# Moving tail loads and zT transposes in SyncE's queue of a fused attention and MLP kernel

## The chip, the cores and the metric

The kernel runs on one core of one Trainium2 chip. The metric is the device time of one execution in microseconds, the median of several runs. The profile is one further execution, recorded by the hardware profiler.

Engines as the profile names them: PE is TensorE (matrix products; PEld are its weight loads), DVE is VectorE, ACT is ScalarE, POOL is GpSimd, SP is SyncE. SyncE computes nothing here: its queue (SPq) issues nearly all DMA transfers, in the order in which they are written. DMA data are moved by 16 DMA engines.

## The reference

Inputs q, k, v have shape (8, 8, 576, 64): batch, heads, sequence, head dimension. All is float32. The output is (8, 576, 512).

```python
scores = scale * np.matmul(q, k.transpose(0, 1, 3, 2))      # scale = 1/sqrt(64)
mask = (rel >= 0) & (rel < 64)                              # rel = query position - key position
attn = softmax(where(mask, scores, -1e9))
x = np.matmul(attn, v)            # heads side by side: (8, 576, 512)
xn = (x - mean) / np.sqrt(var + 1e-6) * g_ln                # over the last axis
out = x + np.maximum(xn @ w_ch1, 0.0) @ w_ch2               # 512 -> 2048 -> 512
```

Each query sees only itself and the 63 keys before it.

## The kernel before, in words

**Blocks and tails.** A batch has 576 rows. Its first 512 are one *block*: blocks 0 to 7, of four sub-blocks of 128 rows (kb 0 to 3). The last 64 rows of two neighbouring batches make one *tail* of 128 rows: tails 0 to 3. The four tails together form a ninth group of 512 rows, number 8 (NGRP - 1), which goes through the MLP like a block.

**Periods.** The main loop (line 963) runs a period g for each of the nine groups. In period g TensorE does the MLP of group g, and between the pieces of that MLP the attention of block b = g + 1 is done and the inputs of block g + 2 are prepared. Period g, from 3 to 6, also does the attention of tail g - 3.

**Units and slots.** The MLP of a period is a list of *units* (`mlp_units`, line 488). In periods 3 to 6 there are 30: units 0 to 15 are layer 1 (four matmuls of 128x512 into a PSUM bank `hps`, then ReLU on ScalarE into `hrT`, line 498); units 16 to 29 are layer 2, computed with seven products of half-size blocks (4, 1, 2, 6, 5, 7, 3; two units each; `product`, line 550, banks pA, pB, pC), whose sums and differences VectorE makes (`s_sums`, line 535). `at(i, f, ...)` puts a step behind unit i; a slot beyond the last (40) means the period's end. The order is written out by hand: all engines take their instructions in this order, and each engine waits at the front of its own queue until what it needs is there. Moving a call moves its instructions within each engine's queue.

**Attention steps.** `s_pe` (line 312) makes the scores of 128 rows on TensorE, `s_exp` the exponential on ScalarE, `s_mask` (360) multiplies by the mask on VectorE, `b_pe` (373) makes the product with v (the tile `xps`), `b_rows` (395) divides by the row sum into `x_norm` (tile `xn`) and takes mean and variance on VectorE, `z_step` (429) normalises to `z` in float16 on GpSimd, and `zt_step` (464) transposes z into `zT`, which layer 1 reads; from block 2 on this is nearly always a DMA transpose from SyncE's queue (470). z has three buffers, so a z that is not transposed yet holds up the third z after it.

**Inputs.** `load_qk` (82), `load_v` (177) and `load_tail` (97) issue loads from SyncE. q and k are cast to float16 on GpSimd (`cast_qk`, 155; in part on ScalarE, `cast_act`, 145) and then transposed: k by TensorE, q of blocks 3 and up by a DMA transpose (`t_main`, 271, line 275). For a tail, `cast_tail` (112) casts tq and tk on GpSimd, `t_tail` (298) issues two DMA transposes into tqT and tkT (302, 303), which the tail's scores read, and `cast_tail_v` (120) casts tv into vt for its product. Loads, transposes and stores share SyncE's queue, so their order in the code is the order in which they are issued.

**Stores.** `store` (532) writes finished rows out from the `xn` buffers: kb 2 and 3 after product 7, kb 0 and 1 after product 3, the last of the period (lines 621 to 634). There are two `xn` tiles to a block and four buffers, so the rows of block g + 2 are written over those of group g: they need its stores to be done.

**The order at the end of a period, before.** At the end of period 4, behind the stores: loads of tail 2's q and k, loads of block 7's q and k; then from slot 2 of period 5: zT of tail 1, the two transposes of tail 2, v of block 7 (first half), tail 2's v, zT of block 6's kb 0.

Of the kernel before, what the change touches and what calls it, by code (L numbers as in the profile page):

```python
# [18 lines left out]
def kernel(  # L19
# [15 lines left out]
    NGRP = B + 1  # L35
# [927 lines left out]
    for g in range(NGRP):  # L963
# [7 lines left out]
        def at(i, f, *a):  # L971
            slots[min(i, len(slots) - 1)].append((f, a))

        def first_scores(b, i):
            at(i, s_pe, b, 0)
            at(i, s_pe, b, 1, False, "xps")
            at(i, s_exp, b, 0, 0, 1)
            at(i + 1, s_exp, b, 1, 0, 1)
            at(i + 1, s_mask, b, 0)
            at(i + 2, s_mask, b, 1)  # L980

        b = g + 1
# [48 lines left out]
        if g == 1:  # L1031
# [38 lines left out]
            for j in range(4):  # L1070
                i = (13, 16, 22, 22)[j]
# [5 lines left out]
                i = (13, 17, 25, 27)[j]  # L1077
# [26 lines left out]
        if g == 2:  # L1104
            at(0, load_qk, 4, 1)
            at(0, s_exp, 3, 1, 1)
            at(1, z_act, 2, 3)
            at(1, s_mask, 3, 1)
            at(2, b_pe, 3, 0)
            at(2, s_pe, 3, 2)  # L1110
            at(2, s_pe, 3, 3, False, "t")
            at(5, zt_step, 2, 3, "act")
            for i, x in zip((2, 3, 4, 6), ((3, 0), (3, 1), (2, 0), (2, 1))):
                at(i, s_exp, 3, *x)
            at(3, load_v, 4, 0, 4)
            at(4, s_mask, 3, 3)
            at(4, b_rows, 3, 0)
            at(4, z_step, 3, 0)
            at(7, s_mask, 3, 2)
            at(7, alloc_qkT, 4)  # L1120
            at(7, after_mask, 3, 2)
            at(7, cast_qk, 4, 0)
            at(7, cast_qk, 4, 1)
            for j in range(1, 4):
                at(9, b_pe, 3, j, ("xps", "t", "sc")[j - 1])
                at((9, 10, 11)[j - 1], b_rows, 3, j)
                at((9, 10, 11)[j - 1], z_step, 3, j)
            for j, i in enumerate((8, 14, 24, 25)):
                at(i, zt_step, 3, j)
        elif g > 1 and b < B:  # L1130
            r, i = NGRP - 1, g - 3
            x, y = (b, 3), (r, i)
            if g > 3:
                at(2, zt_step, r, i - 1)
            at(2, b_pe, b, 0)
            at(2, b_rows, b, 0)
            at(2, z_step, b, 0)
            if g > 4:
                at(2, cast_tail, i)
                at(2, t_tail, i)  # L1140
            if g == 5:
                at(2, load_v, 7, 0, 2)
                at(2, load_tail, 2, "v")
            at(2, s_pe, b, 2)
            at(2, s_exp, b, 2, 0, 1)
            at(3, s_mask, b, 2)
            at(2, s_pe, *x, False, "t")
            at(4, s_exp, *x, 0)
            at(5, s_exp, *x, 1)
            at(5, s_mask, *x)  # L1150
            at(7, b_pe, b, 1)
            at(7, b_pe, *x, "t")
            at(7, b_rows, b, 1)
            at(7, z_step, b, 1)
            at(8, b_rows, *x)
            at(9, z_step, *x)
            at(13, b_pe, b, 2)
            i_s = 13 if g == 6 else 17
            at(i_s, s_pe, *y)
            at(i_s + 2 if g == 6 else i_s, s_exp, *y, 0, 1)  # L1160
            if g == 6:
                at(15, s_mask, *y)
                at(18, b_pe, *y, "sc")
            else:
                at(20, s_mask, *y)
            if g + 2 < B:
                at(5, alloc_qkT, g + 2)
                at(5, after_mask, *x)
                at(5, cast_qk, g + 2, 0)
                at(11, cast_qk, g + 2, 1, (0,))  # L1170
                at(15, cast_act, g + 2, 1, 1)
            for j, w in ((13, (b, 2)), (19, y)) if g == 6 else ((17, (b, 2)),):
                at(j, b_rows, *w)
                at(j, z_step, *w)
            at(2, zt_step, b, 0)
            at(14, zt_step, b, 1)
            if g == 6:
                at(25, zt_step, r, i)
            at(16, zt_step, b, 3)
            at(18 if g == 6 else 17, zt_step, b, 2)  # L1180
        n = g + 2
        if g > 1 and n < B:
            if g > 2:
                at(3, load_v, n, 2, 4)
            at(17, alloc_v, n)
            at(17, cast_v, n, 0, 2)
            at(17, cast_v, n, 2, 4)
            if g == 2:
                at(26, part_vB, n, 0, 4)
            else:  # L1190
                at(17, alloc_vB, n)
                for i, f, c in ((18, vB_cur, 0), (18, vB_prev, 0), (19, vB_cur, 1), (19, vB_prev, 1),
                                (24, vB_cur, 2), (24, vB_prev, 2), (24, vB_cur, 3)):
                    at(i, f, n, c, 0)
            for i, (x, half) in zip((13, 18, 13, 22) if g == 2 else (13, 17, 13, 23),
                                    ((0, 0), (1, 0), (0, 1), (1, 1))):
                at(i, t_main, n, x, half, 0)
            if g > 2:
                at(23, b_pe, NGRP - 1, g - 3, "sc")
                at(23, b_rows, NGRP - 1, g - 3)  # L1200
                at(23, z_step, NGRP - 1, g - 3)
            first_scores(n, 27)
            if n + 1 < B:
                if g == 2:
                    at(40, t_tail, 0)
                elif g == 4:
                    at(40, load_tail, 2, "q")
                    at(40, load_tail, 2, "k")
                at(40, load_qk, n + 1, 0)
                at(40, load_qk, n + 1, 1)  # L1210
                if g == 3:
                    at(40, t_tail, 1)
                if g < 4:
                    at(40, load_v, n + 1, 0, 2)
                if g == 3:
                    at(40, load_tail, 1, "v")
            else:
                for part in "qkv":
                    at(40, load_tail, g - 2, part)
# [4 lines left out]
        if 2 < g < NGRP - 2:  # L1224
            for i in range(1, 5):
                at(7 + i, s_sums, 0, 4, i)
                at((13, 13, 19, 19)[i - 1], s_sums, 4, 6, i)
                at((15, 15, 20, 22)[i - 1], s_sums, 6, 8, i)
        if g in (2, 3):
            for part in "qkv"[:5 - g]:  # L1230
                at(15 if g == 2 else 17, load_tail, g - 2, part)
            at(24, cast_tail, g - 2)
        if 3 <= g < 7:
# [8 lines left out]
        if g in (6, 7):  # L1242
            i = 25 if g == 6 else 24
# [40 lines left out]
```

## Time and profile before

| what | value |
|---|---|
| median of 3 runs | 298.48 us (298.47 to 298.74) |
| the profiled execution, its own time | 299.89 us |
| its span in the profile | 298.2 us |
| mean granted TensorE clock | 0.998 |
| busy share of the span: PE, DVE, ACT, POOL | 97%, 76%, 56%, 55% |
| DMA moved | 57.63 MB in 116,519 packets, mean 193 GB/s |
| packets under 512 B | 86,273 |
| period 4 (first layer 1 matmul to that of the next) | 149.96 to 181.02 us |
| period 5 | 181.02 to 214.08 us |

How to read it: a row of the timeline begins with its start and its length in us, then the engine, the line of the kernel, the operation, the tiles (output <- inputs) and the number of instructions that it merges. Brackets at its end give the time that the engine stood idle before, and what it is taken to have waited for. An SPq row's length is the time that SyncE's queue took to issue; landing comes later, and is read from the table of DMA issues (median us from issue to landing). A row of the windows gives the stretch, its length, busy time and instructions of PE, PEld, DVE, ACT and POOL, the granted clock, the mean busy share of the 16 DMA engines, and GB/s. The share can exceed 1 where transfers overlap in an engine.

### The profile page before, as it was taken

The numbers are of one execution on the slowest core, as the hardware profiler recorded it, in microseconds if no ns is written. First come the engines' busy times: TensorE is split into PE (matmuls) and PEld (weight loads), VectorE is DVE, ScalarE is ACT, GpSimd is POOL, SyncE is SP. The second block draws the span as 40 slices with busy tenths as digits, with TensorE's granted clock in tenths as the row PEclk, the third lists the DMA queues.
The fourth block names the chain that finished last, engine by engine and source line by source line (L and its number), as shares of the span: only waits on it lengthen the run. The fifth ranks groups of instructions, "written<-read, shape, count | busy, mean of one in ns | idle before, by whom it ended". The sixth has DMA issues, their size and how long they took to land.

```text
span 298.2 us, 7942 instructions
## 1 busy us (share of the span) xinstructions
PE 290.0 (97%) x3207; PEld 210.4 (71%) x3207; DVE 226.6 (76%) x435; ACT 168.0 (56%) x284; POOL 164.9 (55%) x243
## 2 busy tenths in 40 slices
PE   8989999999999999999999999999999999999994
PEld 3557545898888888447854786458654888888883
DVE  1782378799994894497757786778989898988983
ACT  2667657677449625768576767658575217305500
POOL 4688866753850885268647491693757543104300
PEclk9999999999999999999999999999999999999999
DMA  7999999969989999899699995999887222003013
GB/s 189 259 381 340 385 286 279 264 213 301 159 180 301 249 155 217 222 312 155 136 294 253 172 157 185 263 216 205 168 203 126 55 73 88 4 0 144 0 37 106
DMA packets 116519, 57.63 MB, mean 193 GB/s; under 512 B 86273, under 2 KB 107841, under 8 KB 116482
## 3 DMA queue, kind: packets, MB, share of 16 engines
q1 hardware_dynamic: 116112, 56.79, 79.7%
q8 instruction: 25, 0.41, 0.6%
q10 hardware_dynamic: 370, 0.33, 0.3%
q14 instruction: 12, 0.10, 0.1%
HBM read 38.80 MB, written 9.44 MB: 162 GB/s over the span
## 4 chain that ended last, share of the span: by engine, by line
PE 82%; DMA 7%; DVE 3%; SPq 3%; issue 2%; ACT 1%; POOL 0%; POOLq 0%; DVEq 0%
PE pA L572 14%; PE hps L498 12%; PE hph L641 12%; PE pB L572 9%; PE pC L572 8%; PE lA L697 5%; PE ch L658 4%; PE xps L392 3%; DMA tkT<-tk 3%; PE sc L345 3%; PE tp L286 3%; PE lC L697 2%; PE warm L887 2%; DMA tk<-in_k_dram 2%; DMA qk<-in_k_dram 2%
## 5 line engine op out<-in xcount | busy, mean ns | idle before, releaser
L498 PE MATMUL hps<-zT,w1g 128*128 128x512 f16 x288 | 65.9, 379 | 0.0
L502 ACT ACTIVATE hrT<-hps 128x512 f16<-128x512 f32 x72 | 43.2, 599 | 25.6 <-PE hps L498 20.7
L572 PEld LDWEIGHTS <-sS 128*128 128x128 f16 x512 | 49.1, 98 | 6.0
L355 ACT ACTIVATE pt<-sc 128x512 f16<-128x512 f32 x72 | 39.5, 601 | 17.2 <-PE sc L345 16.7
L498 PEld LDWEIGHTS <-w1g 128*128 128x128 f16 x288 | 27.0, 98 | 31.0 <-issue 1.5
L572 PEld LDWEIGHTS <-hrT 128*128 128x128 f16 x384 | 36.7, 98 | 6.8 <-ACT hrT L502 0.8
L641 PE MATMUL hph<-zT,w1g 128*128 128x256 f16 x320 | 37.9, 273 | 0.0
L365 DVE TENSOR_TENSOR pt<-pt,mask 128x1024 f16<-128x1024 f16 x32 | 24.6, 776 | 14.6 <-ACT pt L355 14.6
L161 POOL CAST qk<-qk 128x1024 f16<-128x1024 f32 x26 | 28.0, 1087 | 11.7 <-PE sc L345 6.0
L444 POOL TENSOR_SCALAR rsz<-mvg 128x1 f32<-128x1 f32 x32 | 11.8, 368 | 40.8 <-DVE mvg L425 38.2
L641 PEld LDWEIGHTS <-w1g 128*128 128x128 f16 x320 | 30.4, 98 | 4.5 <-ACT w1g L238 0.2
L572 PE MATMUL pC<-w2s,sS 128*128 128x256 f16 x256 | 31.5, 273 | 0.0
L572 PE MATMUL pA<-wT,sS 128*128 128x256 f16 x256 | 30.9, 273 | 0.0
L646 ACT ACTIVATE hrT<-hph 128x512 f16<-128x512 f32 x40 | 24.1, 606 | 10.8 <-PE hph L641 10.6
L714 POOL TENSOR_SCALAR hrT<-hrT 128x512 f16<-128x512 f16 x8 | 12.0, 1503 | 28.6 <-DVE hrT L712 28.6
L416 DVE TENSOR_TENSOR xn<-xps,rcp 128x256 f32<-128x256 f32 (+1 forms) x50 | 25.8, 539 | 1.3 <-DMA out_dram<-xn 0.6
L546 DVE TENSOR_TENSOR sS<-hrT 128x1024 f16<-128x1024 f16 (+2 forms) x39 | 23.3, 598 | 3.5 <-ACT hrT L502 3.4
L422 DVE BATCH_NORM_STATS2 stats<-xn 128x6 f32<-128x512 f32 x36 | 25.0, 694 | 1.2
L450 POOL TENSOR_SCALAR z<-xn,rsz 128x512 f16<-128x512 f32 x24 | 21.7, 905 | 6.7 <-DMA zT<-z 4.2
L267 ACT COPY qkT<-tp 128x1024 f16<-128x1024 f16 (+1 forms) x18 | 17.3, 963 | 14.3 <-PE tp L286 12.1
L445 POOL TENSOR_TENSOR rsz<-rsz,mhalf 128x1 f32<-128x1 f32 x32 | 21.5, 671 | 2.7
L189 POOL CAST vA<-v 128x1024 f16<-128x1024 f32 (+1 forms) x18 | 17.4, 981 | 6.0 <-DMA v<-in_v_dram 5.7
(115 smaller groups left out, 484.6 us busy)
## 6 DMA issues: line engine op xcount, KB each, us to landing
qk<-in_q_dram SPq DMA_DIRECT2D x16, 512.0 KB, 6.0
qk<-in_k_dram SPq DMA_DIRECT2D x16, 512.0 KB, 7.6
out_dram<-xn SPq DMA_DIRECT2D x32, 256.0 KB, 2.8
v<-in_v_dram SPq DMA_DIRECT2D x28, 256.0 KB, 5.9
w2s<-in_moe_w_ch_dram SPq DMA_DIRECT2D x9, 512.0 KB, 8.7
w1s<-in_moe_w_ch_dram SPq DMA_DIRECT2D x4, 512.0 KB, 7.3
tk<-in_k_dram SPq DMA_DIRECT2D x8, 256.0 KB, 4.7
tv<-in_v_dram SPq DMA_DIRECT2D x8, 256.0 KB, 5.8
```

Source lines behind the costliest of these rows:

```text
L161: nc.gpsimd.tensor_copy(out=dst[:, :].rearrange("p (a j) e d -> p a e j d", j=j), in_=t[:, :].rearrange("p (a e j d) -> p a e j d", e=2, j ...
L355: nc.scalar.activation(out=o, in_=i, func=AF.Exp, bias=0.0, scale=scale)
L365: nc.vector.tensor_tensor(out=ptv, in0=ptv, in1=mb, op=ALU.mult)
L416: nc.vector.tensor_tensor(out=xn[:, n * i:n * i + n], in0=xps[:, :, 0:D], in1=rcp_b, op=ALU.mult)
L422: nc.vector.bn_stats(out=stats, in_=xv)
L450: nc.gpsimd.tensor_scalar(out=z, in0=xv, scalar1=rs, scalar2=nm, op0=ALU.mult, op1=ALU.add)
L498: nc.tensor.matmul(out=hps, lhsT=w1g[:, kc, 128 * hc:128 * (hc + 1)], rhs=zT[g][:, kc, :], start=(kc == 0), stop=(kc == NKC - 1),)
L502: nc.scalar.activation(out=hrT[:, hc, :], in_=hps, func=AF.Relu, bias=0.0, scale=1.0)
L546: nc.vector.tensor_tensor(out=o, in0=x, in1=y, op=op)
L572: nc.tensor.matmul(out=o, lhsT=a[:, c, 128 * p:128 * p + 128], rhs=wv[:, c, :], start=(first and (p == 0 or split_c) and c == 0), stop=(c ...
L641: nc.tensor.matmul(out=hps[:, e], lhsT=w1g[:, kc, 128 * hc:128 * (hc + 1)], rhs=zT[g][:, kc, 256 * half:256 * half + 256], start=(kc == 0) ...
L646: nc.scalar.activation(out=hrT[:, 2 * i:2 * i + 2, 256 * half:256 * half + 256], in_=hps, func=AF.Relu, bias=0.0, scale=1.0)
```

## The change

Only the order of steps changes; each instruction stays, with the same shapes.

- Loads of tail 2's q and k: from the end of period 4, behind the stores, to slot 17 of period 4, behind the zT of block 5's kb 2 and ahead of the stores. The cast of tail 2's q and k: from slot 2 of period 5 to slot 24 of period 4. Its transposes: from slot 2 of period 5 to the end of period 4, behind block 7's q and k (in the queue this is the same place but for the zT below).
- zT of tail 0, 1 and 2: from slot 2 of the next period to the end of the own one, right behind the stores and ahead of the q and k loads of the next block (of tail 3's loads in period 5).
- In periods 4 and 5, v of the next block (first half) and the tail's v go behind the zT of kb 0, where they stood ahead of it.
- Period 6: product of block 7's kb 2 and scores of tail 3 from unit 13 to unit 15, exponential still at 15, mask from 15 to 17, product of the tail from 18 to 19, its rows from 19 to 20.

```diff
@@ steps of period g (3 to 6)
-            if g > 3:
-                at(2, zt_step, r, i - 1)
...
-            if g > 4:
+            if g == 6:
                 at(2, cast_tail, i)
                 at(2, t_tail, i)
-            if g == 5:
-                at(2, load_v, 7, 0, 2)
-                at(2, load_tail, 2, "v")
...
-            at(13, b_pe, b, 2)
-            i_s = 13 if g == 6 else 17
+            at(15 if g == 6 else 13, b_pe, b, 2)
+            i_s = 15 if g == 6 else 17
             at(i_s, s_pe, *y)
-            at(i_s + 2 if g == 6 else i_s, s_exp, *y, 0, 1)
+            at(i_s, s_exp, *y, 0, 1)
             if g == 6:
-                at(15, s_mask, *y)
-                at(18, b_pe, *y, "sc")
+                at(17, s_mask, *y)
+                at(19, b_pe, *y, "sc")
...
-            for j, w in ((13, (b, 2)), (19, y)) if g == 6 else ((17, (b, 2)),):
+            for j, w in ((15, (b, 2)), (20, y)) if g == 6 else ((17, (b, 2)),):
                 at(j, b_rows, *w)
                 at(j, z_step, *w)
             at(2, zt_step, b, 0)
+            if g in (4, 5):
+                at(2, load_v, g + 2, 0, 2)
+                at(2, load_tail, i, "v")
@@ the end of period g
+            if g > 2:
+                at(40, zt_step, NGRP - 1, g - 3)
             if n + 1 < B:
                 if g == 2:
                     at(40, t_tail, 0)
-                elif g == 4:
-                    at(40, load_tail, 2, "q")
-                    at(40, load_tail, 2, "k")
                 at(40, load_qk, n + 1, 0)
                 at(40, load_qk, n + 1, 1)
-                if g == 3:
-                    at(40, t_tail, 1)
-                if g < 4:
+                if g > 2:
+                    at(40, t_tail, g - 2)
+                else:
                     at(40, load_v, n + 1, 0, 2)
-                if g == 3:
-                    at(40, load_tail, 1, "v")
...
-        if g in (2, 3):
-            for part in "qkv"[:5 - g]:
+        if g in (2, 3, 4):
+            for part in "qkv"[:3 if g == 2 else 2]:
                 at(15 if g == 2 else 17, load_tail, g - 2, part)
             at(24, cast_tail, g - 2)
```

## The prediction

> **What bounds the kernel now.** I read the page first, then TensorE's timeline for periods 4 and 5, then SyncE's and GpSimd's rows in the same stretch, then the windows.
>
> ```profile
> span 298.2 us, 7942 instructions
> PE 290.0 (97%) x3207; PEld 210.4 (71%) x3207; DVE 226.6 (76%) x435; ACT 168.0 (56%) x284; POOL 164.9 (55%) x243
> ```
>
> TensorE is busy for 97%, so only its idle time can be won without taking work away. The timeline shows where that is:
>
> ```profile
> 149.96 2.78 PE L498 MATMUL hps<-zT,w1g 128*128 128x512 f16 x12
> 168.13 0.41 PE L345 MATMUL sc<-tqT,tkT 64*128 64x64 f16 x16
> 174.71 0.45 PE L392 MATMUL xps<-vt,pt 128*64 128x65 f16 x16
> 181.02 2.78 PE L498 MATMUL hps<-zT,w1g 128*128 128x512 f16 x12
> 200.12 0.41 PE L345 MATMUL sc<-tqT,tkT 64*128 64x64 f16 x16 [0.58 <-DMA tkT<-tk]
> 207.04 0.45 PE L392 MATMUL xps<-vt,pt 128*64 128x65 f16 x16 [0.28 <-DVE xn L585]
> 211.70 0.53 PE L345 MATMUL sc<-qkT,qkT 64*128 64x64 f16 x24 [0.38 <-DMA qkT<-qk]
> 214.08 2.79 PE L498 MATMUL hps<-zT,w1g 128*128 128x512 f16 x12
> 229.09 0.41 PE L345 MATMUL sc<-tqT,tkT 64*128 64x64 f16 x16 [0.43 <-DMA tkT<-tk]
> ```
>
> The hps rows open periods 4, 5 and 6. Period 4 takes 181.02-149.96 = 31.06 us, period 5 takes 33.06 us for the same matmuls: 2.00 us to win. Laying one on the other: 0.27 up to unit 13 (VectorE's mask took 0.97 us at 188.72, 0.69 at 157.66), 0.65 at tail 2's scores, 0.34 at its vt product, 0.57 at block 7's scores, 0.16 at the end (period 6's first matmul waits for zT). Period 6 waits 0.51 more for tail 3's keys. The vt wait is charged to VectorE, but GpSimd's cast of vt ended at 206.98, after 4.12 us of waiting for tv.
>
> ```profile
> 173.41 4.32 SPq L470 DMA_TRANSPOSE zT<-z  x3
> 180.05 2.70 SPq L533 DMA_DIRECT2D out_dram<-xn  x4
> 182.80 1.32 SPq L107 DMA_DIRECT2D tq<-in_q_dram  x2
> 184.17 2.38 SPq L110 DMA_DIRECT2D tk<-in_k_dram  x2
> 186.59 1.18 SPq L92 DMA_DIRECT2D qk<-in_q_dram  x1
> ```
> ```profile
> 193.74 2.60 SPq L303 DMA_TRANSPOSE tkT<-tk  x1
> 197.79 3.64 SPq L110 DMA_DIRECT2D tv<-in_v_dram  x2
> 204.90 3.46 SPq L275 DMA_TRANSPOSE qkT<-qk  x2
> ```
> ```profile
> 175.00:180.00 5.00, 5.00 (x81) 4.29 (x76) 4.08 (x9) 3.56 (x6) 4.32 (x7) 1.00 0.47 105
> 200.00:205.00 5.00, 4.88 (x62) 4.42 (x63) 4.16 (x10) 4.78 (x8) 1.52 (x3) 1.00 1.44 203
> ```
>
> SyncE's one queue serves all this. It stands idle from 177.73 to 180.05, held at the stores, while the DMA share (next to last column) is 0.47; from 182.80 it works without a pause, and at 200 to 205 the share is 1.44. Everything late in period 5 is late in this one line.
>
> **The change, part by part.**
>
> *Tail 2's q and k before the stores of period 4.* Four issues (1.32 + 1.25 to 2.38 us) move from behind the stores to behind zT of block 5's block 2. I put that zT's end at 178.1 (next paragraph), so they take the idle SyncE time to 180.7 or 181.8. The first two stores go from 180.05 to about 180.8, the second two still wait for VectorE until 181.94. What followed, block 7's q and k, started at 186.59; now it starts at 182.8 plus one moved zT (1.3 to 1.9 us), 184.1 to 185.2. If DMA throughput, not issue, is the limit, the same backlog of stores and tail starts at 178.1 instead of 180.05: 1.95 us. I take this smaller shift for all that comes later. GpSimd's casts of tail 2 (0.61 and 1.04 us) now stand ahead of block 6's z_0; keys issued at 180.1 land 5.2 us later (the tk row) and are cast by 186.4, about when z_0's statistics are there (186.10): z_0 is late by 0.3 at most, and SyncE asks for it only at 192.
>
> *zT of the tail's rows behind the stores.* In period 4 its z was ready at 148.06, in period 5 about 180.1: no wait. It delays q and k of the next block by its issue, counted above. *zT of the first block ahead of v.* Period 4: two transposes of 1.5 us each now go ahead of v6 and tv1, which start 3 us later; tv1 lands at 172.0 instead of 169.1 (issued at 164.30, 4.8 to land), its cast ends at 173.3, and the vt product starts at 174.71: hidden, with 1.4 us left, else its lateness is paid. In return GpSimd's wait of 4.24 us at 169.79 (z for a buffer that this zT holds) goes; tv1 becomes the next late thing, so z of block 2 ends about 0.4 us later, 176.0, which is where 178.1 comes from. Period 5: it adds 0.6 us of transfer ahead of tv2 and nothing ahead of the transposes of block 7, which it already preceded.
>
> *What period 5 wins*, with the shift of 1.95: tail 2's keys land at 200.07-1.95 = 198.1, wanted at 168.13+31.06 = 199.2 (199.5 if the slow mask stays): 0.65 won. tv2 (second issue at 199.66 at the latest, 5.8 to land) arrives about 205.4-1.95+0.6 = 204.1, is cast in 1.3 by 205.4, and is wanted at 174.71+31.06 = 205.8: 0.34 won. qkT of block 7 lands at 211.6-1.95 = 209.65, wanted at 178.69+31.06 = 209.8: as close as the estimate can tell, 0.50 of 0.57. zT at the end: 0.12 of 0.16. The slow mask had tail 2's q cast beside it on GpSimd (188.54); the cast moves to about 183, z_0 takes its place: 0.14 of 0.27. Sum 1.75; ends 0.65 and 2.00.
>
> One page speaks on that last term. The Trainium skill (SBUF — State Buffer, Who interferes with whom) says that a VectorE instruction with two SBUF inputs contends with a GpSimd one that reads SBUF. The two overlapping rows agree; by it 0.27 would be won if z_0 is over by 188.72, and nothing if not.
>
> *Period 6's tail at unit 15.* Two units are eight matmuls, 1.74 us of cover. But TensorE comes 1.75 us earlier into period 6, and tail 3's loads do not: they follow stores that wait for VectorE, which has two sums of w1 between (1.42 and 1.45 us), so the stores come 1.1 us earlier, and the zT now in front takes 1.3 to 1.7 back. tkT of tail 3 lands near 228.9 as before (229.03); TensorE asks at 228.58+1.74-1.75 = 228.6. The wait falls from 0.51 to about 0.35. Against it, VectorE gets fuller: the mask before 222.5 and the product of the tail four units later (five before), now behind the mask of unit 17, may wait 0.1 to 0.2. Net 0; bounds -0.6 (the next rows with VectorE behind) and +0.51. Periods 7 and 8 show no idle TensorE, and zT of block 7 is due 0.8 us before its use: cost 0, up to 0.5 if it is late.
>
> The profiled execution took 299.89 us, 1.69 outside its span of 298.2; it lies 1.41 above the median of 298.48. The sum makes the span 296.45, and the median 298.48-1.75 = 296.7.
>
> **The rivals.**
>
> *The stores are late and hold VectorE: slower.* Block 6's first rows are written at 184.47 into the buffer that the first two stores of period 4 read. VectorE then has an idle 2.0 us (to 188.72, the mask that TensorE needs at 189.75), so a store that lands after 186.5 delays TensorE one for one. Issued at 181.2 or 182.2. Nearest rows: stores issued 2 us behind tail 1's loads landed in 3.6 us, 184.8 to 185.8, no loss; the zT that stood right behind four q and k loads took 7.5 us, 188.7 to 189.7: 2.2 to 3.2 lost. It decides from a landing at 188.9; at the far end 298.48-1.75+3.2 = 299.9. The Trainium skill (DMA: Bandwidth & Descriptors, Queues, rings and completion order) speaks for it: each engine takes descriptors in ring order, and the completion count lands after every earlier write from that engine. The 7.5 us row agrees; by it the store lands no earlier than tk, at 185.3, which is still in time.
>
> *The backlog only changes its order.* If v and the transposes gain nothing, only tail 2's keys are won: 298.48-0.65 = 297.8. The 1.44 share speaks for it, the 0.47 window against it.
>
> *tv1 late in period 4.* 1.4 us of margin on a landing known to some 1.5: costs up to 1.0, 297.7.
>
> *All waits go, period 6's too:* 298.48-2.5 = 296.0.
>
> *Nothing moves:* another wait takes the place of each, 298.5.
>
> **How the numbers follow.** Forecast 296.7 (296.2 to 297.2): 0.52. All waits go: 0.10. Order only, or tv1 late, 297.2 to 297.9: 0.18. No change within 0.2% (0.6 us, about what a measurement can tell): 0.07. Late stores or a new wait in periods 6 to 8, above 299.1: 0.13. So faster 0.80, same 0.07, slower 0.13. The range 295.9 to 298.4 leaves out the slower case and a little of the others.
>
> **What would show it.** Right: period 5 lasts 31.1 to 31.7 us between hps rows, tail 2's scores have no wait, tq and tk are issued between 177 and 182, GpSimd's 4.2 us wait for zT is gone, and period 6 still waits for tkT. Wrong: a row of VectorE's xn waiting for out_dram near 185, a TensorE wait at the vt product of period 4, or the excess of period 5 coming back at block 7's scores or in period 7.

## The result

The changed kernel takes 297.36 us (median of 5 runs, 297.17 to 297.60), the kernel before 298.48 us (298.08 to 299.10): a ratio of 0.996, 95% interval 0.9945 to 0.9975. It is faster by 1.12 us. The forecast was 296.7 in a range of 295.9 to 298.4. Medians and ranges, here and in the experiments, leave out three much longer executions (301.54, 304.31 and 1466.72 us) in which the mean granted clock was lower (0.992, 0.949 and 0.187).

The profiled execution of the changed kernel took 297.58 us, 2.31 less than the profiled one of before (299.89), twice the difference of the medians. The experiments below deal with that first. Its page:

```profile
span 295.9 us, 7944 instructions
PE 288.8 (98%) x3207; PEld 210.2 (71%) x3207; DVE 226.8 (77%) x435; ACT 168.2 (57%) x284; POOL 165.6 (56%) x243
```

TensorE's timeline, the rows that answer to those shown of before (start, length, instruction, tiles; a bracket would be a wait):

```profile
181.28 2.78 PE L498 MATMUL hps<-zT,w1g 128*128 128x512 f16 x12
199.45 0.41 PE L345 MATMUL sc<-tqT,tkT 64*128 64x64 f16 x16
206.03 0.45 PE L392 MATMUL xps<-vt,pt 128*64 128x65 f16 x16
212.35 2.78 PE L498 MATMUL hps<-zT,w1g 128*128 128x512 f16 x12
228.57 0.41 PE L345 MATMUL sc<-tqT,tkT 64*128 64x64 f16 x16
232.58 0.45 PE L392 MATMUL xps<-vt,pt 128*64 128x65 f16 x16
```

Period 5 lasts 212.35-181.28 = 31.07 us, as period 4 does: all 2.00 us of excess over period 4 are gone, the wait for tail 3's keys in period 6 too. No row has a bracket: behind 46 us this execution shows no wait of TensorE. SyncE's queue:

```profile
173.38 4.72 SPq L470 DMA_TRANSPOSE zT<-z  x3
178.14 1.29 SPq L107 DMA_DIRECT2D tq<-in_q_dram  x2
179.48 1.25 SPq L110 DMA_DIRECT2D tk<-in_k_dram  x2
180.82 3.11 SPq L533 DMA_DIRECT2D out_dram<-xn  x4
184.03 1.35 SPq L470 DMA_TRANSPOSE zT<-z  x1
185.43 1.47 SPq L92 DMA_DIRECT2D qk<-in_q_dram  x1
```

Tail 2's loads stand in the time in which SyncE was idle, and block 7's q starts at 185.43 instead of 186.59. The windows have TensorE busy all of 200 to 205, and the DMA share there fell from 1.44 to 1.06:

```profile
175.00:180.00 5.00, 5.00 (x86) 4.31 (x86) 4.00 (x10) 3.48 (x6) 3.77 (x6) 1.00 0.54 119
200.00:205.00 5.00, 5.00 (x52) 4.51 (x50) 4.80 (x10) 4.36 (x7) 2.06 (x3) 1.00 1.06 215
```

The price shows on VectorE, in the row that the prediction named as a sign of being wrong:

```profile
186.00 0.69 DVE L416 TENSOR_TENSOR xn<-xps,rcp 128x512 f32<-128x512 f32 x1 [1.30 <-DMA out_dram<-xn]
```

It waits 1.30 us for the stores, and TensorE loses nothing by it, since VectorE has more slack than that here.

### The profile page after: what moved, and what is told of

Read it like the earlier page. It is cut to its first block, busy times and chain, and to the rows that moved or that the text cites. A ratio compares the mean times of both kernels' runs of the same rounds, so it can differ in the third digit from the quotient of the medians.

```text
span 295.9 us, 7944 instructions
## 1 busy us (share of the span) xinstructions
PE 288.8 (98%) x3207; PEld 210.2 (71%) x3207; DVE 226.8 (77%) x435; ACT 168.2 (57%) x284; POOL 165.6 (56%) x243
## 4 chain that ended last, share of the span: by engine, by line
PE 74%; DMA 11%; POOL 4%; SPq 4%; DVE 3%; issue 2%; ACT 1%; POOLq 0%; ACTq 0%
PE hps L498 14%; PE pA L572 12%; PE hph L641 10%; PE pB L572 9%; PE pC L572 8%; DMA qk<-in_k_dram 6%; PE lA L697 5%; PE xps L392 3%; DMA w2s<-in_moe_w_ch_dram 3%; PE sc L345 3%; PE tp L286 3%; PE lC L697 2%; DMA tv<-in_v_dram 2%; PE ch L510 1%; PE lB L697 1%
## 5 line engine op out<-in xcount | busy, mean ns | idle before, releaser
L546 DVE TENSOR_TENSOR sS<-hrT 128x1024 f16<-128x1024 f16 (+2 forms) x39 | 24.6, 631 | 4.0 <-ACT hrT L502 3.9
L445 POOL TENSOR_TENSOR rsz<-rsz,mhalf 128x1 f32<-128x1 f32 x32 | 20.8, 651 | 2.7
L189 POOL CAST vA<-v 128x1024 f16<-128x1024 f32 (+1 forms) x18 | 16.5, 935 | 6.6 <-DMA v<-in_v_dram 6.4
```

Source lines behind the costliest of these rows:

```text
L546: nc.vector.tensor_tensor(out=o, in0=x, in1=y, op=op)
```

## The experiments

All were timed in rounds beside the kernel before on the same chip; the three groups (the first four, the next four, the last four) have medians of before of 299.07, 298.83 and 299.22 us. Ratios are to these.

| run | median, us (range) | ratio to before, 95% interval |
|---|---|---|
| before again | 299.12 (298.03 to 300.54) | 1.0006 (0.9987 to 1.0025) |
| tail 2 early, alone | 297.48 (297.21 to 298.71) | 0.9947 (0.9928 to 0.9965) |
| zT moves alone | 300.62 (299.67 to 301.61) | 1.0051 (1.0030 to 1.0073) |
| unit 15 alone | 299.15 (297.89 to 300.45) | 1.0012 (0.9991 to 1.0033) |
| changed kernel again | 297.21 (297.12 to 297.91) | 0.9947 (0.9927 to 0.9966) |
| changed, zT not moved | 297.28 (297.05 to 298.74) | 0.9953 (0.9937 to 0.9968) |
| changed, tail at unit 13 | 297.80 (297.20 to 298.85) | 0.9961 (0.9944 to 0.9978) |
| changed, tail 2's v early too | 299.60 (298.50 to 301.60) | 1.0029 (1.0006 to 1.0051) |
| tails' zT alone | 300.04 (299.45 to 302.39) | 1.0047 (1.0025 to 1.0068) |
| first block's zT alone | 299.55 (299.08 to 301.67) | 1.0022 (1.0004 to 1.0041) |
| changed, tails' zT back | 297.92 (296.86 to 299.79) | 0.9968 (0.9945 to 0.9992) |
| changed, tail 2 between the stores | 299.36 (298.31 to 300.76) | 1.0008 (0.9990 to 1.0025) |

### The kernel before, once more

No edit.

> The kernel before once more, unchanged. Theory 1 (the waits of periods 5 and 6 differ from execution to execution, because landings differ, and the profiled execution of before was one with long ones): the median stays within 0.3 us of 298.5, and a profiled execution near that median shows a period 5 of 31.5 to 32.5 us and waits of TensorE in periods 5 and 6 of 0.7 to 1.6 us together, not 2.5. Rival (the waits are the same in each execution, and the 1.4 us by which the profiled one lay above the median are elsewhere, so that the changed kernel gives 1.2 us back somewhere): period 5 takes 33.0 to 33.1 us again and period 6 waits 0.5, whatever the span.

Measured: its runs reach from 298.03 to 300.54 us, and the runs of before beside it from 297.79 to 300.67. The profiled execution took 298.39 us, near the first median. TensorE's timeline:

```profile
181.26 2.78 PE L498 MATMUL hps<-zT,w1g 128*128 128x512 f16 x12
200.07 0.41 PE L345 MATMUL sc<-tqT,tkT 64*128 64x64 f16 x16 [0.29 <-DMA tkT<-tk]
206.65 0.45 PE L392 MATMUL xps<-vt,pt 128*64 128x65 f16 x16
213.05 2.78 PE L498 MATMUL hps<-zT,w1g 128*128 128x512 f16 x12
227.57 0.41 PE L345 MATMUL sc<-tqT,tkT 64*128 64x64 f16 x16
```

The same program has a period 5 of 213.05-181.26 = 31.79 us here, against 33.06, and no wait for tail 3. The excess of periods 5 and 6 over period 4 is 0.73 us together, against 2.51; the difference of 1.78 is a little more than that of the two times, 1.50. Of the 0.73, 0.29 are the wait in the row and 0.29 the slow mask (0.98 us). So the waits are not a property of the program alone: they depend on landings that differ from execution to execution (tail 2's second tv landed 4.7 us after its issue here, 5.8 in the first profile). Theory 1 fits, though 0.73 is at the lower edge of what it expected and the median, 299.12, lies above the 298.8 that it allowed. The rival falls: nothing is given back elsewhere.

### The parts, each alone

Tail 2's loads and casts early, nothing else:

```diff
-                elif g == 4:
-                    at(40, load_tail, 2, "q")
-                    at(40, load_tail, 2, "k")
...
-        if g in (2, 3):
-            for part in "qkv"[:5 - g]:
+        if g in (2, 3, 4):
+            for part in "qkv"[:3 if g == 2 else 2]:
```

> Only tail 2's q and k loaded and cast in layer 2 of period 4; zT and period 6 as before. Theory 1: the tail's transposes and all behind them come about 2 us earlier, so period 5 takes 31.1 to 31.6 us and the time is 0.6 to 1.1 us below before; period 6 still waits up to 0.5 for tail 3. Rival (the backlog only changes its order): only the wait at tail 2's scores goes, tv and the transposes of block 7 stay late, period 5 takes 32 us or more and the time falls by at most 0.4.

Measured 297.48 us, 1.6 below before: more than expected, since the kernel before took 299.07 on this chip. The rival falls. The profiled execution was the slowest of its runs (298.71), and it shows something of use. Its VectorE row at the stores, then its TensorE rows:

```profile
187.63 0.69 DVE L416 TENSOR_TENSOR xn<-xps,rcp 128x512 f32<-128x512 f32 x1 [3.12 <-DMA out_dram<-xn]
```
```profile
181.10 2.78 PE L498 MATMUL hps<-zT,w1g 128*128 128x512 f16 x12
190.50 0.22 PE L392 MATMUL xps<-vB,pt 128*64 128x65 f16 x1 [0.77 <-DVE pt L365]
200.23 0.41 PE L345 MATMUL sc<-tqT,tkT 64*128 64x64 f16 x16
213.12 2.78 PE L498 MATMUL hps<-zT,w1g 128*128 128x512 f16 x12
227.88 0.41 PE L345 MATMUL sc<-tqT,tkT 64*128 64x64 f16 x16 [0.20 <-DMA tkT<-tk]
```

This is the rival of late stores. The stores began at 181.51 behind tail 2's loads, VectorE waited 3.12 us for them, and TensorE 0.77 for the mask behind VectorE's wait. Period 5 took 32.02 us, more than the 31.1 to 31.6 that theory 1 expected, and 0.77 of the excess of 0.96 is this wait. Tail 2's keys are no longer late.

The zT moves alone (the two `zt_step` and the `load_v`, `load_tail` lines of the diff):

> Only the zT transposes moved (tails' behind the stores, first block's ahead of v); tail 2's loads and period 6 as before. GpSimd's 4.2 us wait for zT in period 4 goes. If that wait does not matter for TensorE (both theories): no change, -0.3 to +0.3 us, and tail 2's keys are still waited for 0.3 to 1.0 us, since one more transpose stands ahead of block 7's q and k. If it is the true source of the lateness in period 5: 0.5 us or more faster.

Measured 300.62 us, 1.5 slower: outside what was expected, which was no change. GpSimd's wait of 4.2 us for zT in period 4 did go, but nothing was won by it. The profiled execution is the longest of its runs (301.61 us); in period 5, with one row of the windows below:

```profile
201.53 0.41 PE L345 MATMUL sc<-tqT,tkT 64*128 64x64 f16 x16 [2.04 <-DMA tkT<-tk]
216.04 2.78 PE L498 MATMUL hps<-zT,w1g 128*128 128x512 f16 x12
```
```profile
203.00:205.00 2.00, 2.00 (x11) 1.43 (x10) 0.00 (x0) 1.98 (x4) 0.24 (x2) 0.50 1.34 213
```

Period 5 began at 181.24 and took 34.80 us, 3.73 more than period 4 (31.07). TensorE's wait for tail 2's keys is 2.04 of it. The other 1.69 are matmuls that ran slower behind this wait: the granted clock, 1.00 up to it, was 0.61 from 201.5 to 203, 0.50 from 203 to 205, 0.94 from 205 to 207 and then 1.00 again, which loses 1.5*0.39 + 2*0.50 + 2*0.06 = 1.70 us. The median run has a mean clock of 1.0, so its 1.5 us are not explained by this.

Period 6's tail at unit 15, alone (the lines of the diff for `g == 6`):

> Only period 6's tail at unit 15. TensorE reaches period 6 as late as before, so the 1.74 us of added cover hide tail 3's keys: its wait (0.51 us in the first profile, 0.0 to 0.5 by theory 1 in a typical execution) goes and nothing takes its place: 0.0 to 0.5 us faster. Rival (VectorE is now the bound of layer 2 in period 6): the wait moves to the tail's product with v, no change or up to 0.3 us slower.

Measured 299.15 us, no difference that shows; the interval reaches from 0.3 us faster to 1.0 slower, so the time alone does not decide between the two. In the profiled execution (299.80) tail 3's keys are not waited for, but its product is, since the mask comes late from VectorE:

```profile
230.33 0.41 PE L345 MATMUL sc<-tqT,tkT 64*128 64x64 f16 x16
234.79 0.46 PE L392 MATMUL xps<-vt,pt 128*64 128x65 f16 x16 [0.46 <-DVE pt L365]
```

So in this execution the rival is right: the wait moved to the product.

### The changed kernel, with one part undone

> The changed kernel once more, beside the next three. If the waits that differ from execution to execution are what it removes, its runs spread less than those of before (297.8 to 300.7 in the last 33) and the gain against that larger set is 1.4 to 1.9 us, more than the 1.1 of the first five runs.

Measured: 297.12 to 297.91 us beside 298.05 to 300.69 of before, a gain of 1.62 us (298.83 to 297.21) at a ratio of 0.9947. The spread of before is nearly gone in these six runs, as expected. Its profiled execution, the slowest of the six at 297.91, has a period 5 of 31.44 us; the 0.38 of excess lie ahead of tail 2's scores, at VectorE's mask:

```profile
188.94 1.07 DVE L365 TENSOR_TENSOR pt<-pt,mask 128x1024 f16<-128x1024 f16 x1 [1.39 <-ACT pt L355]
```
```profile
188.71 0.77 POOL L450 TENSOR_SCALAR z<-xn,rsz 128x512 f16<-128x512 f32 x1
```

The mask takes 1.07 us: GpSimd's z was still running as it began, and it ends 0.53 us behind z (the last section has more such rows). In the first profile of the changed kernel z came after the mask (189.91), and the mask took 0.69.

All zT back where they were:

> The changed kernel with all zT where they were before (tail 2 early and unit 15 kept). Theory 2 (zT ahead of v in period 4 is what lets SyncE reach tail 2's loads in time, and so the stores behind them land in time): GpSimd waits 4 to 5.5 us for zT in period 4 again, tail 2's loads start 0.7 us later, VectorE waits 2.5 to 3.5 us for out_dram near 185 in the profile, TensorE up to 0.8; in time 0.1 to 0.6 us slower than the changed kernel. Rival (zT only costs, as it did alone): same or up to 0.5 us faster than the changed kernel.

Measured 297.28 us: within 0.1 of the changed kernel. GpSimd's wait for zT came back (4.4 us), VectorE's for out_dram was 1.04 and TensorE lost no more than 0.1 us. With tail 2's loads early, the zT moves are worth nothing that shows; theory 2 is not confirmed, and what they cost when made alone is gone as well.

Period 6's tail back at unit 13:

> The changed kernel with period 6's tail at unit 13 again. Tail 3's keys land near 227 in the profile of the changed kernel, and unit 13 would ask at 226.8: a wait of 0.0 to 0.6 us for tkT in period 6, and the time 0.0 to 0.5 us above the changed kernel's. Had my prediction of step 6 been right (keys at 228.9): a wait of about 2 us, 1.5 to 2 us slower.

Measured 297.80 us, 0.6 above the changed kernel, with intervals that overlap. In the profiled execution (297.41) the tail's scores stand at 226.60, and TensorE stood idle for less than 0.1 us before them. The keys landed at 226.6 (issued at 223.40, landed 3.2 us later), just as they were asked for, so the 228.9 of the prediction is refuted; a gain by unit 15 is possible, not shown.

### More in front of the stores, and less

Tail 2's v, too, ahead of the stores, on top of the changed kernel:

```diff
-                at(2, load_tail, i, "v")
+                if g == 4:
+                    at(2, load_tail, i, "v")
...
-            for part in "qkv"[:3 if g == 2 else 2]:
+            for part in "qkv"[:2 if g == 3 else 3]:
```

> The changed kernel with tail 2's v, too, loaded ahead of the stores of period 4: 0.5 MB more in front of them. This makes the suspected cost of the change larger. If stores land only after the loads issued ahead of them, VectorE's wait for out_dram near 186 grows from 1.3 us to 3.5 to 5, its 2 us of slack are used up, and TensorE waits 1.5 to 3 us for the mask near 190: the kernel 1 to 3 us slower than the changed one. If stores overtake the loads: a wait of 1 to 2 us as now, and no change in time (tv is then early enough).

Measured 299.60 us, 2.4 slower than the changed kernel and 0.8 slower than before. The profiled execution was the fastest of its runs (298.50), so it shows less of the loss than the median run had; VectorE and TensorE:

```profile
187.79 0.69 DVE L416 TENSOR_TENSOR xn<-xps,rcp 128x512 f32<-128x512 f32 x1 [3.50 <-DMA out_dram<-xn]
```
```profile
180.88 2.78 PE L498 MATMUL hps<-zT,w1g 128*128 128x512 f16 x12
190.66 0.22 PE L392 MATMUL xps<-vB,pt 128*64 128x65 f16 x1 [1.15 <-DVE pt L365]
213.27 2.79 PE L498 MATMUL hps<-zT,w1g 128*128 128x512 f16 x12
```

3.50 us of wait on VectorE make 1.15 on TensorE, and period 5 has 32.39 us. The first store landed only after the loads ahead of it: at 185.9 (issued at 181.47, landed 4.4 us later), behind the second tv at 185.2 (180.43, 4.8). It is the same in the changed kernel (185.3, behind tk at 184.6) and with tail 2 early alone (186.0, behind 185.4). The slack is 3.50-1.15 = 2.35 us (3.12-0.77 = 2.35 in the execution above). The wait of 1.30 in the changed kernel has 1.05 left.

Tail 2's q and k between the two pairs of stores:

```diff
-                at(15 if g == 2 else 17, load_tail, g - 2, part)
-            at(24, cast_tail, g - 2)
+                at({2: 15, 3: 17, 4: 27}[g], load_tail, g - 2, part)
+            at(28 if g == 4 else 24, cast_tail, g - 2)
```

> The changed kernel with tail 2's q and k issued between the two pairs of stores of period 4 instead of ahead of both (cast in slot 28). The first pair no longer stands behind loads, so VectorE's wait for out_dram near 186 goes (0 to 0.3 us); SyncE's idle time before the stores is not used, and the loads start at 181, 3 us later. If what is won comes from that idle time: tail 2's keys are waited for 0 to 0.5 us, 0.1 to 0.8 us slower than the changed kernel. If being ahead of block 7's q and k by 1.7 us more is enough: the same or faster, with a smaller spread.

Measured 299.36 us: the whole gain is lost, more than expected. The wait for out_dram is gone, and the waits of before are back (profiled execution 299.28 us):

```profile
199.90 0.41 PE L345 MATMUL sc<-tqT,tkT 64*128 64x64 f16 x16 [0.63 <-DMA tkT<-tk]
207.30 0.45 PE L392 MATMUL xps<-vt,pt 128*64 128x65 f16 x16 [0.75 <-POOL vt L124]
214.00 2.79 PE L498 MATMUL hps<-zT,w1g 128*128 128x512 f16 x12
```

Its loads started at 180.94 instead of 178.14. The later cast is not what holds the keys: GpSimd stood idle for 2.86 us until tk landed and cast it at 188.86. So the gain comes with the 2.3 us of SyncE's idle time in front of the stores, not with being ahead of block 7's q and k alone.

### Which zT costs

The kernel before with only the tails' zT moved, and with only the first block's:

> The kernel before, with only the tails' zT moved behind the stores. Moving all zT alone lost 1.5 us, at tail 2's keys. If it is this transpose that loses it (in period 5 it now stands ahead of tail 2's loads and block 7's q and k, where it stood behind them): 0.8 to 1.6 us slower than before, wait for tkT 0.8 to 2.0. If not: within 0.4 of before.

> The kernel before, with only the first block's zT moved ahead of v. In period 5 tail 2's transposes stand ahead of both, so their keys cannot come later by it: within 0.4 us of before if the tails' zT is what lost 1.5 us. If instead v and tv coming later is the cause: 0.8 us or more slower, with waits at the vt product or at block 7's scores.

Measured 300.04 and 299.55 us, 0.8 and 0.3 slower than before; both intervals lie above 1, so both cost something, and the first probably more (the intervals overlap). SyncE's queue with the tails' zT moved (the longest of its runs, 302.39 us):

```profile
182.61 1.22 SPq L470 DMA_TRANSPOSE zT<-z  x1
183.88 2.17 SPq L107 DMA_DIRECT2D tq<-in_q_dram  x2
186.09 1.25 SPq L110 DMA_DIRECT2D tk<-in_k_dram  x2
```

The transpose takes 1.22 us of queue, and tk is issued at 186.09 instead of 184.17. Tail 2's keys, already late, come later still: TensorE waits 2.60 us for them, more than the 2.0 expected, and behind this wait too the granted clock falls to 0.50 (201.6 to 203), so this execution is not a typical one. In the run with the first block's zT (299.43 us) TensorE waits 0.91 for tkT, no more than executions with the order of before show (0.29 to 0.95), and 0.55 for vt, the latter behind tv2.

With the tails' zT put back in the changed kernel:

> The changed kernel with the tails' zT back in slot 2 of the next period; the first block's zT stays ahead of v. If the tails' zT only delays what is behind it: block 7's q and k and tail 3's loads start 1.3 us earlier, and nothing waited in the changed kernel, so the time is the same within 0.3 us, or up to 0.3 lower by a smaller spread. If the z buffer that it holds matters (a wait of GpSimd for zT comes back): 0.2 us or more slower.

Measured 297.92 us, 0.7 above the changed kernel, with a wide range (296.86 to 299.79) and an interval that overlaps that of the changed kernel. The profiled execution (298.95) has GpSimd waiting for zT again (0.9 us in two waits) and TensorE 0.41 for vt. That the buffer of z is the cause fits, but the run doesn't show it apart from the rest. No version tried is faster than the changed kernel by a clear margin.

## Why the prediction was right, and where it was off

*The forecast of faster by 0.6%, and the main mechanism: right.* Period 5 was to take 31.1 to 31.7 us: it took 31.07 and 31.44 in two executions. Tail 2's loads were to be issued between 177 and 182: 178.14 to 180.73. The three landings that the sum rests on came out close: tail 2's keys at 197.3 (198.1 forecast), its second tv at 203.8 (204.1), block 7's qkT at 209.4 (209.65). The part that does it is this one; alone it wins 0.53%, and without SyncE's idle time it wins nothing.

*The size: 1.78 predicted, 1.12 measured, then 1.62.* The step that failed is the last of the sum, "the median 298.48-1.75". It took waits that were summed in one execution off the median of others. The profiled execution of before held 2.51 us of this excess, the execution near the median 0.73. In the profile the gain was larger than the forecast (2.31 us, for 1.75), in the first five runs smaller. The median of before is no fixed number either: 298.48 in five runs, 298.8 to 299.2 in the larger sets. So 297.36 lies in the band that the prediction gave to "order only, or tv1 late" (297.2 to 297.9), but the traces show neither: v and the transposes came earlier as well, and tv1 was in time.

*Period 6 was to keep a wait of 0.35 for tail 3: wrong.* The mis-sized term is the landing of tk, 6.3 us after its issue in before. In the changed kernel SyncE and GpSimd show:

```profile
217.42 1.44 SPq L110 DMA_DIRECT2D tk<-in_k_dram  x2
218.90 2.08 SPq L110 DMA_DIRECT2D tv<-in_v_dram  x2
223.92 1.24 SPq L303 DMA_TRANSPOSE tkT<-tk  x1
```
```profile
222.85 1.04 POOL L118 CAST tk<-tk 128x1024 f16<-128x1024 f32 x1 [1.00 <-DMA tk<-in_k_dram]
```

The second tk landed 4.4 us after its issue (the table of DMA issues), and its cast began at 222.85. Besides, the zT that stood between tv and the tail's transposes before (222.80, 1.69 us) was counted where it now stands in front, but not for what its move frees behind: tkT went out as the cast ended, at 223.92, where before it went out 0.46 us behind the cast's end. The keys landed at 227.1, not 228.9, and the scores asked at 228.57. The balance of the period, net 0, was 0.5 too low in this execution.

*Late stores, the rival on the other side: the mechanism is real.* It was priced at a slack of 2.0 us and a landing of 3.6 to 7.5. The slack is 2.35; in the changed kernel the first two stores landed 4.5 and 3.7 us after their issue (the table of DMA issues), the second at 185.9, and cost 1.30 of it. In two other executions it is used up, and TensorE loses 0.77 and 1.15 us. The Trainium skill (DMA: Bandwidth & Descriptors, Queues, rings and completion order) says that a transfer's completion count lands only after every earlier write of the same DMA engine; the landings of the stores behind the loads agree. The sign of being wrong that the prediction named, a row of xn waiting for out_dram near 185, was too strict: the row appeared and cost nothing, and only a wait beyond the slack would have.

*The slow mask, 0.14 of 0.27: right as a coin toss.* It stands between two outcomes that both came: all of it won, or 0.10 lost. The mask took 0.69 us in one execution of the changed kernel and 1.07 in the other, against 0.97 before, by where GpSimd's z fell: behind the mask where the stores had held VectorE, and so z, for 1.30 us, beside it where they had held it for 0.69. The rule of the Trainium skill (SBUF — State Buffer, Who interferes with whom) agrees with both.

*zT: "no wait", its issue counted above.* Right in the changed kernel. That the same moves cost 0.3 to 1.5 us where tail 2's loads stay behind the stores was not foreseen: the issue of 1.2 us was counted, but not that it then falls on a chain that is already late, nor that a wait of 2 us lowers the clock behind it.

*tv1 in period 4:* GpSimd waited 3.38 us for it, its cast stood at 171.27, 0.7 earlier than I had it land, and the vt product at 174.96 did not wait. Hidden, as taken.

## What to carry to other kernels

Look for the time in which an in-order DMA queue stands held at an instruction that isn't ready, and put transfers that are ready in front of it: 2.3 us of such time were worth 1.6 us here, while the same loads one place further back were worth nothing. What is then held behind them must have slack of its own; read it from the waiting engine's row and make the load larger once to see where it ends. Before a sum of waits is taken off a median, look at a second execution: the wait for tail 2's keys was three times as long in one execution as in another with the same instructions up to there (0.95 and 0.29 us).

## What was not expected of the hardware

The same program took 297.79 to 300.67 us in 33 runs on one chip, while the changed kernel stayed within 297.12 to 297.91 in its 11 runs, six of them on another chip. In the executions that were profiled the difference sits in landings: with the same instructions ahead of it, tail 3's second tk took 6.3, 5.1 and 5.8 us to land, and TensorE waited 0.58, 0.29 and 0.95 us for tail 2's keys (before, before again, unit 15 alone).

Behind a wait of 2.04 us the granted clock of TensorE fell to 0.50 and took about 3.4 us to come back, which cost 1.7 us on top of the wait (zT moves alone); behind 2.60 us it fell as well (tails' zT alone). Behind the waits of up to 1.15 us in the other executions it stayed at 1.00. Nothing here lies between 1.15 and 2.04.

A mask on VectorE (both operands in SBUF, 128x1024) takes 0.66 to 0.69 us alone. Where a wide GpSimd instruction (a cast or z) had begun more than 0.1 us ahead of it and had more than 0.2 us left, the mask ended 0.53 to 0.55 us behind the end of that instruction, as if it had waited for it. This holds for all 75 such masks in the 14 profiles: 0.97 us beside the cast of tq (before), 1.07 beside z (changed kernel again), 1.52 beside a cast of qk (at 70.92 in before). GpSimd's instructions on 128x1 tiles did not lengthen it. Where the mask began first it kept its 0.69, and z took 1.22 us instead of 0.77 (changed, zT not moved: mask at 188.59, z at 188.70).
